# A new table for the order, the engines and the PSUM banks of all operations in a one-core recurrence and convolution kernel

## The chip, the core and the metric

The kernel runs on one core of a Trainium2 chip. The metric is the time of one execution on the device in microseconds, the median over runs. In the text PE is the matrix engine, DVE, ACT and POOL are the vector, scalar and general engines, and SP is the engine that issues the DMAs.

## The reference

Two stages, with the output of the first as the input of the second. B = 4 batches, S = 6272 steps, D = 256 channels, all in float32.

```python
def _attn_ref(x, f_logit, lower_bound):
    sig = 1.0 / (1.0 + np.exp(-f_logit))
    f = lower_bound + (1.0 - lower_bound) * sig
    h = 0
    for t in range(S):
        h = f[:, t] * h + (1.0 - f[:, t]) * x[:, t]
        y[:, t] = h

def _moe_ref(x, w_proj, filter_fft, w_out):
    x1, x2, x3 = split(x @ w_proj)                      # three times D columns
    X2 = np.fft.rfft(x2, axis=1)
    H = np.fft.rfft(filter_fft, axis=0)
    x2_conv = np.fft.irfft(X2 * H, axis=1)              # circular, of length S
    return (x1 * x2_conv * x3) @ w_out
```

## The kernel before

The Fourier transform of length 6272 = 49 x 128 is done in matmuls in two steps, with tables of sines and cosines that are computed on the chip at the start. The work of a batch has these operations; the name of an operation is the first argument of `op(...)` in the code, and the line is that of its matmul or of its main instruction.

- `load` (L308): the DMAs of 512 steps of f_logit (tile FL) and x (tile XT), 512 KB each; 13 chunks a batch, each tile with three buffers. `sig` (L311, ACT) makes the sigmoid, `u` (L313, POOL) the product with x, `su` (L325, PE) transposes both, in two operations of 16 transposes for a full chunk, `f` (L338 on ACT, L340 on DVE) makes the gate, and `scan` (L346, DVE) runs the recurrence along the chunk. `wrap` copies a part of the result for the circular access.
- `P` (L673, PE): the projection to x2 from strided columns of the recurrence's output, 13 groups; it needs all scans of the batch. `x2` evicts it.
- `F1` (L686), `mini` (L702), `F2` (L745): the two steps of the forward transform, in 16 units; `A` evicts F1, `prod` (L758, DVE) multiplies by the filter's spectrum, of which `H` (L723) loads one unit, and `slot` and `zm` do the first bin. `I2` (L768) is the first step back, and `Th` evicts it.
- `x13` (L373): 52 projections to x1 and x3, evicted by `xs`, and multiplied by `z` (L389, POOL).
- `I1` (L802): the last step back, 13 groups, which needs all `Th`; `y` (L808, DVE) multiplies by z; `proj` (L820) is the output projection, `o` evicts it, and `store` (L830) writes 512 KB.

Before the first batch the filter's own spectrum is made: 13 loads `ff`, casts `fr`, `rot` (L590), evictions `f2`, 32 `FF1` (L615) evicted by `afs`, 16 `FF2` (L633) evicted by `hw`, and stores `hst` to DRAM. The tables need two blocks of DVE work and two sines on ACT, all named `args` (L479 to L521). There are 32 operations `warm` (L561), each of four matmuls on a constant whose output is read by nothing; an operation `warm` needs only the constant and one PSUM bank.

While a batch is in F1 to I2, the scans of the next one begin; after the last I2 they go on beside I1, y and proj, and P of the next batch follows. "Cycle" b is the time from the first P of batch b to that of batch b+1.

No scheduler runs at build time. `Plan` collects 2325 operations with what they read and write; `ORDER` is a string of base-64 digits, three for each operation, in the order in which they are issued. The order on each engine, and so all waiting, follows from it: engines run their own queue in order, and semaphores hold an operation until those that it needs are done. All DMAs stand in one queue, SP's. PSUM is one tile of eight banks; the table says which bank, or pair of banks, an operation takes, and its evictions take the same.

```python
word = a * 4096 + b * 64 + c
yield word // 64, self.ENGINES[word // 8 % 8], word % 8     # operation, engine, bank
...
assert e in o["cost"] and i not in seen and o["preds"] <= seen
```

Operations with more than one engine in their `cost` (evictions, copies, gates, casts) may be given to any of these by the table.

## Time and profile before

| | |
|---|---|
| median of 3 runs | 476.47 us (476.25 to 478.01) |
| span of the profiled execution, first to last instruction | 476.4 us |
| PE busy | 447.8 us, 94% |
| DVE, ACT, POOL busy | 424.9, 416.1, 297.9 us |
| DMA | 112.88 MB, 237 GB/s on average |
| first P of batches 0, 1, 2, 3 | 78.7, 178.3, 282.7, 386.6 us |
| last F2 of batches 0, 1, 2, 3 ends | 143.6, 239.8, 346.3, 443.4 us |

The profiled execution has no separate time beside its span, which is within 0.1 us of the median, so sums may be made against either. Busy time of PE counts matmuls whose ends are modelled; a stretch in which PE is busy throughout can still hold short waits between matmuls. "Idle before" of a group is the idle time of its engine ahead of its instructions, with what ended most of it.

### The profile page before, as it was taken

How to read it: one execution, taken by the hardware profiler on the slowest of the kernel's cores; microseconds unless marked ns; L12 is line 12 of the kernel's file. 1: busy time of each engine (PE TensorE's matmuls, PEld its weight loads, DVE VectorE, ACT ScalarE, POOL GpSimd, SP SyncE). 2: the span in 40 equal slices, each digit the busy share in tenths (PEclk: the TensorE clock that was granted, in tenths of full speed). 3: DMA queues.
4: the chain of work that ended last, by engine and by line, in shares of the span. 5: the costliest groups of instructions: out<-in, count | busy, mean ns of one | idle time of the engine just before them, and what ended most of it. 6: DMA issues, size and time to landing. Idle time of an engine off the chain costs nothing.

```text
span 476.4 us, 14713 instructions
## 1 busy us (share of the span) xinstructions
PE 447.8 (94%) x6041; PEld 345.4 (72%) x6041; DVE 424.9 (89%) x457; ACT 416.1 (87%) x606; POOL 297.9 (63%) x309
## 2 busy tenths in 40 slices
PE   8888999999998999999999999999999799999995
PEld 7776777866756879776666889666767697676784
DVE  8778989799999996999999996999999877999874
ACT  5899898899999998889999978999999778999763
POOL 6777784287889730668798734688787504766600
PEclk9999999999999999999999999999999999999999
DMA  8989998636588897157769995567588831356277
GB/s 329 396 310 317 313 342 251 227 104 216 165 289 306 289 328 279 41 164 226 244 230 312 345 338 219 145 205 235 163 271 270 341 135 46 110 152 193 77 279 277
DMA packets 39841, 112.88 MB, mean 237 GB/s; under 512 B 4258, under 2 KB 6178, under 8 KB 39774
## 3 DMA queue, kind: packets, MB, share of 16 engines
q1 hardware_dynamic: 39774, 111.94, 69.0%
q8 instruction: 47, 0.77, 0.6%
q14 instruction: 20, 0.16, 0.1%
HBM read 80.93 MB, written 31.00 MB: 235 GB/s over the span
## 4 chain that ended last, share of the span: by engine, by line
PE 52%; DVE 16%; DMA 12%; POOL 6%; ACT 6%; issue 6%; SPq 0%; ACTq 0%; DVEq 0%; POOLq 0%
PE PS L373 13%; PE PS L673 9%; DVE HA L346 8%; PE PS L768 8%; PE PS L745 6%; PE PS L686 5%; DVE ys L808 5%; PE PS L325 4%; DMA XT<-in_x_dram 4%; DMA X<-in_moe_filter_fft_dram 4%; PE PS L820 3%; POOL zt L389 3%; POOL XT L313 3%; DMA out_dram<-osb 2%; DVE PP L758 2%
## 5 line engine op out<-in xcount | busy, mean ns | idle before, releaser
L389 POOL TENSOR_TENSOR zt<-x1s,x3s 128x490 f16<-128x490 f32 (+1 forms) x104 | 125.5, 1214 | 67.1 <-ACT x3s L270 33.0
L313 POOL TENSOR_TENSOR XT<-XT,FL 128x1024 f32<-128x1024 f32 (+1 forms) x52 | 116.9, 2248 | 64.7 <-ACT FL L311 41.8
L758 DVE TENSOR_TENSOR PP<-PS,Hu 98x1008 f16<-98x1008 f32 x128 | 146.5, 1198 | 4.9 <-PE PS L745 2.7
L346 DVE TENSOR_TENSOR_SCAN HA<-fTs,HA,PS 128x512 f16<-128x512 f32 (+1 forms) x96 | 112.5, 1201 | 5.1 <-ACT fTs L338 4.3
L373 PE MATMUL PS<-HA,W 128*128 128x490 f16 (+1 forms) x416 | 104.5, 368 | 1.3 <-ACT Th L270 0.6
L808 DVE TENSOR_TENSOR ys<-PS,zt 128x1024 fp32r<-128x1024 f32 (+1 forms) x52 | 58.8, 1150 | 8.5 <-PE PS L802 6.5
L820 PE MATMUL PS<-Wo,ys 128*128 128x256 f32 x392 | 57.8, 293 | 3.5 <-DVE ys L808 2.5
L270 ACT CAST HA<-PS 128x1024 f16<-128x1024 f32 x57 | 57.2, 1025 | 3.7 <-PE PS L686 3.6
L338 ACT ACTIVATE fTs<-PS,nomc 128x512 f32<-128x512 f32 (+1 forms) x86 | 56.2, 672 | 4.8 <-PE PS L325 4.3
L272 ACT ACTIVATE osb<-PS 128x1024 f32<-128x1024 f32 (+1 forms) x46 | 45.0, 985 | 16.9 <-DMA out_dram<-osb 8.7
L768 PEld LDWEIGHTS <-PP 98*128 98x128 f16 x1024 | 49.7, 98 | 11.7 <-POOL PP L750 2.1
L270 ACT COPY x3s<-PS 128x490 f32<-128x490 f32 (+1 forms) x96 | 54.6, 574 | 4.0 <-PE PS L373 1.8
L820 PEld LDWEIGHTS PS<-Wo,ys 128*128 128x128 f32 x392 | 49.3, 188 | 9.0 <-DVE ys L808 4.6
L272 ACT ACTIVATE x1s<-PS 128x490 f32<-128x490 f32 (+1 forms) x89 | 52.1, 592 | 3.9 <-PE PS L373 2.2
L373 PEld LDWEIGHTS <-W 128*128 128x128 f16 x416 | 33.4, 97 | 30.4 <-issue 8.3
L311 ACT ACTIVATE FL<-FL 128x1024 f32<-128x1024 f32 (+1 forms) x52 | 52.8, 1019 | 2.1 <-DMA FL<-in_f_logit_dram 2.0
L325 PE MATMUL PS<-iden,FL 64*128 64x64 f32 x784 | 45.8, 232 | 8.6 <-DVE HA L346 2.2
L325 PEld LDWEIGHTS PS<-iden,FL 64*128 64x128 f32 x784 | 33.7, 138 | 27.0 <-DVE HA L346 9.0
L768 PE MATMUL PS<-VA,PP 98*128 98x98 f16 x512 | 51.8, 207 | 0.6 <-POOL PP L750 0.2
L270 ACT CAST Th<-PS 128x784 f16<-128x784 f32 x61 | 50.2, 830 | 1.8 <-PE PS L768 1.2
L768 PE MATMUL PS<-VB,PP 98*128 98x98 f16 x512 | 51.6, 207 | 0.0
L673 PE MATMUL PS<-W,HA 128*128 128x256 f16 x392 | 44.6, 274 | 0.2 <-DVE HA L346 0.2
(110 smaller groups left out, 685.7 us busy)
## 6 DMA issues: line engine op xcount, KB each, us to landing
FL<-in_f_logit_dram SPq DMA_DIRECT2D x48, 512.0 KB
XT<-in_x_dram SPq DMA_DIRECT2D x48, 512.0 KB
out_dram<-osb SPq DMA_DIRECT2D x48, 512.0 KB
Hu<-H SPq DMA_DIRECT2D x55, 392.0 KB
X<-in_moe_filter_fft_dram SPq DMA_DIRECT2D x9, 512.0 KB
H<-Hu SPq DMA_DIRECT2D x16, 196.0 KB
H<-Hu SPq DMA_DIRECT2D x16, 128.0 KB
Hu<-in_moe_filter_fft_dram SPq DMA_DIRECT2D x2, 512.0 KB
```

Source lines behind the costliest of these rows:

```text
L270: nc.scalar.copy(dst, src)
L272: nc.scalar.activation(dst, src, AF.Copy, scale=scale)
L313: op("u", {"POOL": 0.1 + 0.553 * nb}, lambda e, xt=xt, ft=ft: nc.gpsimd.tensor_tensor(xt, xt, ft, op=AOP.mult), r=[("ft", k)], w=[("xt", k)])
L325: nc.tensor.transpose(bank(pb)[:, at[p] + j:at[p] + hn:nb], src[ps, j, cols], iden[ps, ps])
L346: nc.vector.tensor_tensor_scan(h, fT, bank(pb)[:, 512 - hn:512 + hn], init, op0=AOP.mult, op1=AOP.add),
L373: nc.tensor.matmul(PS[:, p, 0:n], W13[:, kh, js], HA[:, HB[kh] + t0:HB[kh] + t0 + n], start=(kh == 0), stop=(kh == 1))
L389: nc.gpsimd.tensor_tensor(late["zt"][:, jb, :, m0:m0 + nm], xs(0), xs(1), op=AOP.mult),
L673: nc.tensor.matmul(pp[:, r - r0, :], column(HB[kh], q_of(r)), W2[:, kh, :], start=(kh == 0), stop=(kh == 1))
L758: nc.vector.tensor_tensor(PP[:TB, k, o, :, :, 1:64], px.unsqueeze(1).broadcast_to([TB, 2, UE, 63]), hh[:, :, :, 1:64], op=AOP.mult)
L768: nc.tensor.matmul(PS[:, ib + o, pr * TB:(pr + 1) * TB], PP[:TB, k, o, n, 2 * pr:2 * pr + 2, :], v[:TB], start=(n == 0), stop=(n == 1))
L808: nc.vector.tensor_tensor(late["ys"][:, yk, :, 0:rn * 128], PS[:, cb:cb + 2, 0:rn * 128], late["zt"][:].rearrange("p k r m -> p k (r m)") ...
L820: nc.tensor.matmul(po[:, i, :], late["ys"][:, yk, kh, i * 128:(i + 1) * 128], Wo[:, kh, :], start=(kh == 0), stop=(kh == 1))
```

## The change

The string `ORDER` is replaced; every other line is the same (the file is two lines shorter, so that a line of the code after the table has a number smaller by 2).

```diff
 ORDER = (
-    "A8gAAYBBgAOYABIAjQBLgACIBGgAtRBQgBVgAhSBagBkgAdTA7YAPIAxUBfgA9AA2VBpgAwWBCAA0XBugBDQA+SBFABMYBzgAyUBEAARIAvV"
-    "BHYBACAqWA/CBNUA1XAQAB4gAmQERgBIRBWYAkWAcTBRAADgAYYAuXAnQBJBAgWBKBESgBSWAzTBUGBbYBXQBTGEpgAeSBYIBgYASABcSBPE"
...
+    "AAYAOYABIA7YBBgBCAA1QAfQA8gA9YAuQBLgA2QBGgBVgBQgBfgBagA5QBkgBpgBugAkQACIBDQBzgBMYA+SBFABHYBEAAPIAQAAVYAXYATIAUIB"
+    "NQBPAAWIBWIA/CBOIBIUBRABJEBKMB4gBXWBZGBgABAKBYGBSQBUABTABbIBhSBiKBqYAYYBcUBeEBlIBmQBnIBoABvIBrWBdMBjCBwQB0IByIBt"
...
 )
```

Decoded, the two tables hold the same 2325 operations. 149 of them change their engine, by kind:

| operation | engines before | engines after |
|---|---|---|
| A (F1's eviction) | ACT 57, DVE 7 | ACT 58, DVE 6 |
| Th (I2's eviction) | ACT 61, DVE 3 | ACT 63, DVE 1 |
| afs, f2, hw (start-up's evictions) | ACT 53, DVE 22 | ACT 53, DVE 22 |
| f (gate) | ACT 86, DVE 18 | ACT 91, DVE 13 |
| fr (start-up's casts) | POOL 8, ACT 4, DVE 1 | POOL 5, ACT 3, DVE 5 |
| o (output's eviction) | ACT 46, DVE 6 | ACT 51, DVE 1 |
| wrap | POOL 31, ACT 17 | POOL 43, ACT 5 |
| x2 (P's eviction) | ACT 33, DVE 19 | ACT 27, DVE 25 |
| xs (x13's eviction) | ACT 185, DVE 23 | ACT 182, DVE 26 |

1352 of the operations with banks get other banks. In the order over all engines the median operation moves by 15 places. The largest moves are those of `warm`: all 32 stood ahead of the first P; now 8 do, 20 stand between the first P and the last projection, and 4 behind that. On PE the order of su, I1, proj, F1, F2, I2 and x13 among each other changes throughout; two x13 that stood ahead of the first P come behind it. The second `args` block of DVE and the second sine of ACT come later in the start-up: the sine now stands behind the sigmoid of chunk 11, where a table load precedes it and another precedes the sigmoid that follows. On SP the input loads, the filter's stores and the spectrum's loads are ordered a little differently.

## The prediction

> **What bounds the kernel now.** I read the page first (parts 1, 2, 4), then the sums of busy time in stretches cut where the P phase of each batch begins and where its last F2 ends (times from the matmuls of L673 and L745), then the groups by form, then the timelines of the load loop and of the first 15 us.

> ```profile
> span 476.4 us, 14713 instructions
> ...
> PE 447.8 (94%) x6041; PEld 345.4 (72%) x6041; DVE 424.9 (89%) x457; ACT 416.1 (87%) x606; POOL 297.9 (63%) x309
> ...
> PEclk9999999999999999999999999999999999999999
> ...
> PE 52%; DVE 16%; DMA 12%; POOL 6%; ACT 6%; issue 6%; SPq 0%; ACTq 0%; DVEq 0%; POOLq 0%
> ```

> PE is the bound, with DVE close behind. By stretches (P to last F2, then last F2 to next P; batches 0 to 3):

> ```profile
> 91.20:143.60 52.40, 51.22 (x711) 34.55 (x709) 49.85 (x53) 49.88 (x79) 41.76 (x42) 1.00 0.62 197
> 143.60:178.30 34.70, 31.68 (x558) 26.43 (x559) 34.33 (x34) 32.55 (x49) 24.57 (x20) 1.00 0.90 305
> ...
> 239.80:282.70 42.90, 39.83 (x668) 31.34 (x663) 41.82 (x41) 40.02 (x61) 32.32 (x25) 1.00 0.87 304
> ...
> 346.30:386.60 40.30, 36.07 (x597) 29.23 (x596) 37.97 (x37) 33.93 (x51) 25.15 (x21) 1.00 0.79 281
> ```

> Columns: length, then PE, PEld, DVE, ACT, POOL busy, granted clock, DMA share, GB/s. The first row is PE-bound. In the other three DVE is busy for 34.3 of 34.7, 41.8 of 42.9 and 38.0 of 40.3 us, and PE idles 3.0, 3.1 and 4.2: scans of the next batch and y products set the pace there. The first 78.7 us (before the first P) are a start-up of their own, with DMA at a share of 0.87 to 0.96 in its 20 us windows.

> **What the change does, counted from the two tables.** No arithmetic is added. 149 operations change engine. Priced by the medians of the rows without waits, DVE's sum goes from 421.5 to 420.2 us, ACT's from 400.5 to 397.2, POOL's from 291.7 to 295.4 (12 wraps at 0.52 leave ACT). No engine's total matters to 0.5%; the order does. Four parts:

> **1. Warm-up matmuls.** Of 32 warm groups (L561) the old table has all before the first P; the new has 8 there, 4 behind the last projection, and 20 in between: 8, 4 and 8 in the three cycles from P to P, 7 of these ahead of a last F2 and 13 behind one.

> ```profile
> 8.70 1.48 PE L561 MATMUL PS<-iden 128*128 128x256 f16 x12
> ```

> Twelve take 1.48 us with the last one's own 0.27 us; so four cost (1.48-0.27)/11 x 4 = 0.44 us. 20 x 0.44 = 8.8 us more PE work after the first P. The four at the end (1.8 us) lie beside the last eviction and store: the last projection ends at 471.5 and the span at 476.4, so they cost nothing up to 4.9 us.

> **2. PE work that moves.** Between P and P the old table's matmuls, at gapless durations (x13 0.42, P 0.87, F1 0.46, F2 0.54, I2 0.70, I1 0.55, proj 1.14, su 0.62 us per operation), sum to 92.9, 98.4 and 96.2 us, and 83.1 in the last cycle: 370.6. The measured lengths are 99.6, 104.4, 103.9 and 89.8 = 397.7; take off 4.9 for the tail and PE's lost time is 22.2 us. The new table moves two x13 from the start-up into cycle 0 (+0.8) and one proj from cycle 3 to 2 (zero in sum): 97.3, 100.2, 100.8 and 82.0 without the end's warm groups = 380.3, so +9.7 with the warm groups. All of PE's order stands behind each other, so this is paid in full unless PE waits become fewer.

> **3. Waits that become fewer.** (a) The load loop: XT and FL have three buffers, so chunk c+3 is loaded only when chunk c has been transposed.

> ```profile
> 129.60 0.42 PE L325 MATMUL PS<-iden,XT 64*128 64x64 f32 x8
> 129.86 0.67 SPq L308 DMA_DIRECT2D FL<-in_f_logit_dram  x1
> ...
> 135.04 1.05 ACT L311 ACTIVATE FL<-FL 128x1024 f32<-128x1024 f32 x1
> ...
> 137.04 2.36 POOL L313 TENSOR_TENSOR XT<-XT,FL 128x1024 f32<-128x1024 f32 x1
> ...
> 139.37 0.47 PE L325 MATMUL PS<-iden,FL 64*128 64x64 f32 x8
> ```

> From 130.0 to 139.4: 9.4 us for load, sigmoid, product. The same loop takes 9.3 to 9.7 us for batch 1, about 10 for batch 2, about 11 for batch 3. PE work between the transposes of c and c+3 was 7.8, 8.1, 7.8, 7.1, 7.7 us for chunks 3 to 7 of batch 1; in the new table it is 11.1, 10.8, 10.2, 8.4, 8.6 (its warm groups among it, so they are counted once). What is short moves all that follows on PE: 1.7 at chunk 3 and 2.4 at chunk 6 make 4.1 us; with 1.5 and 2.1 for batches 2 and 3 (leads of 8.8 to 10.1) 7.7 in all. New: 1.1 + 0.3 + 1.1 = 2.5 us. (b) One-eviction waits: for each PE group I took the PE work since the group that filled its banks, or produced its operand, against the duration of that eviction plus 0.25 us (an estimate: an eviction starts about 0.04 us behind its matmul, PE about 0.06 behind its releaser, and the last matmul's own tail). Groups that fall short: 59 in the old, by 17.8 us in sum; 37 in the new, by 11.4 (0.9 of it warm groups). The gain is mostly between last F2 and next P, where the order of I1, y, proj and su is wider. The old 22.2 us = 7.7 + k x 17.8 gives k = 0.81; the new is 2.5 + 0.81 x 11.4 = 11.7, so -10.5 us. If none of it comes: 0. If lost time goes no lower than the queue work of DVE allows (the DVE queue from P to P sums to 90.7, 98.1 and 97.0, under PE's), this bound does not bite.

> **4. Start-up.** Up to its last gate, ACT's queue goes from 61.4 us and 3 table loads to 59.4 and 5, because the second sine is now queued late, between the sigmoids of chunks 11 and 12; behind it wait the last gates and so the last scans, which P needs.

> ```profile
> L521 ACT ACT_TABLE_LOAD x1 | 1.3, 1283 | 0.0
> ...
> L521 ACT ACTIVATE PP<-PP 128x512 f32<-128x512 f32 x1 | 0.7, 652 | 0.0
> ```

> 65.3 against 65.8 us with the loads; DVE 67.6 to 66.9, POOL 56.3 to 56.1, bytes ahead of the last input load one H store (0.13 to 0.2 MB) fewer. I take 0. Below: casts on POOL are 5 rather than 8 and DVE's second argument block (8.1 to 14.1 us) comes behind the casts, so FF1 (now at 24.3) can begin up to 2.5 us sooner. Above: the two loads and the sine at the late place, 3.2 us, plus 0.8 for the scans behind them: +4. [...]

> SP has the same 259 transfers and one queue; H loads and stores keep their order within a few places, with bytes unchanged: zero, its cover being DMA shares of 0.60 to 0.90 in these stretches.

> **Sum.** 476.4 + 9.7 - 10.5 + 0 = 475.6 us; the profiled span is within 0.1 of the median 476.47, so 475.6 is also the forecast of the median. A measurement of this kernel tells about 0.5% (2.4 us) from no change: faster is under 474.1, slower over 478.9.

> **Rivals.**
> PE pays, and nothing comes back. The place: last F2 to next P, where the new PE queue holds 33.1, 35.6 and 37.8 us of work and DVE's, with two products ahead, 32.1, 35.1 and 36.2 (old: PE 30.9, 39.2, 35.7; DVE 34.0, 41.5, 35.2). PE is then the bound in all three, and two equal queues wait for each other: in the old third stretch, where they are equal, 40.3 us were needed, 4.6 over the larger. The price is 0.44 us a warm group and part 2, +9.7: 486.1 us. It decides if the lost 22 us stay within 5 us of what they were. For it: lost PE time was near 6 to 8 us in each cycle, whatever the cycle's work. Against it: the loop's 9.4 us explain 4 of them.
> Waits shrink and the warm groups also fall into idle time: of the 13 behind a last F2, half (2.9 us) fit into the 10.3 us that PE idles there, and the head of the start-up gives its 2.5; with a quarter of the 9.2 us of eviction waits that I left in (0.81 x 11.4; 2.3 us): 475.6-2.9-2.5-2.3 = 467.9 us. Against it: the shortfalls already count warm groups as filler.
> The clock. The first 32 matmuls of L561 took 6.57 us, 0.205 each, against 0.11 at 8.70: PE began at half speed, and the record shows full speed from 7.3 us on. With 24 groups gone, PE between 7 and 24 us has little but 13 rotations of 0.58 us. If the clock falls and FF1, FF2 and su run at half speed until it rises, 6.8 us of PE work (24 to 32 us) doubles; half is covered by loads: +3.4, 479.0 us. [...]

> **Chances.** Forecast 0.42 (472 to 480: a third of it is faster, half the same, the rest slower); PE pays 0.30; more hidden 0.22; clock 0.06 (a third the same). Faster 0.14 + 0.22 = 0.36; same 0.22 + 0.02 = 0.24; slower 0.06 + 0.30 + 0.04 = 0.40. The range reaches from 467 (the third case's end) to 486 (the second's), leaving a tenth out on each side. The likeliest case is one of both signs; its own range is 472 to 480.

> **What would show it.** Right: the first P at 76 to 82 us; P to P lengths of about 100, 104 and 104 us with PE's idle time before su (L325) and I1 (L802) falling; five ACT table loads of 1.28 us; L561 rows at 120 to 410 us without idle time before them. Wrong: last F2 to next P longer than 34.7, 42.9 and 40.3 in sum; P to last F2 longer by over 5 us in sum than 246.8; granted clock under 1.00 between 8 and 32 us; or a start-up outside -2.5 to +4, which this working would not explain.

## The result and the profile after

| | before | after |
|---|---|---|
| median (range), us | 476.4 (476.25 to 478.01) | 483.1 (481.07 to 484.75) |
| span of the profiled execution, us | 476.4 | 479.3 |
| first P of batches 0 to 3 | 78.7, 178.3, 282.7, 386.6 | 81.4, 183.0, 286.8, 389.2 |
| last F2 of batches 0 to 3 ends | 143.6, 239.8, 346.3, 443.4 | 149.2, 250.4, 352.5, 446.0 |
| last projection ends | 471.5 | 474.3 |

The new table is slower: ratio 1.013, interval 1.0098 to 1.0162. The forecast was 475.6 us; its range (467 to 486) holds the result, its sign does not.

One thing must be known before the two profiles are compared. After's profiled execution took 481.07 us at a span of 479.3, and in every run that lists both, the time is 1.7 to 2.1 us above the span (1.9 to 2.0 for the kernel before). Before's span of 476.4 therefore fits its run of 478.01 us, not its median, as the prediction had it. So the profiles compare before's slowest run with after's fastest, and show 2.9 us (spans) of the 6.7 us between the medians. Where in the kernel the other 3.8 us lie no profile shows; the experiments below are judged by their medians.

The page of after:

```profile
span 479.3 us, 14704 instructions
...
PE 451.9 (94%) x6041; PEld 351.6 (73%) x6041; DVE 425.4 (89%) x457; ACT 415.2 (87%) x599; POOL 303.1 (63%) x318
...
PEclk9579997999999999999999999999999999999999
...
PE 60%; DVE 12%; ACT 10%; DMA 6%; POOL 6%; issue 4%; SPq 1%; ACTq 0%; DVEq 0%; POOLq 0%
```

PE is still the bound, and holds more of the chain (60% for 52%). The clock row is new: it falls in slices 2 and 3 (12 to 36 us) and again in slice 7 (72 to 84 us). Before had full speed from 7.3 to 474.9 us.

The stretches of after, P to last F2 and last F2 to P (columns as in the prediction):

```profile
81.40:149.20 67.80, 66.41 (x854) 49.51 (x854) 58.13 (x59) 62.96 (x93) 43.99 (x46) 0.98 0.65 209
149.20:183.00 33.80, 32.96 (x565) 27.19 (x560) 33.26 (x32) 31.15 (x46) 25.40 (x20) 1.00 0.85 304
...
250.40:286.80 36.40, 35.32 (x604) 29.64 (x602) 35.99 (x36) 32.73 (x49) 28.09 (x24) 1.00 0.84 302
...
352.50:389.20 36.70, 36.60 (x608) 30.66 (x604) 36.27 (x35) 32.08 (x48) 24.09 (x19) 1.00 0.75 279
```

Last F2 to next P, where the prediction looked for its gain, did shrink: 106.9 us in sum for 117.9. P to last F2 grew by as much: 257.7 for 246.8. From the first P to the last projection nothing is won or lost. The same stretch in one window, first before, then after:

```profile
78.70:471.50 392.80, 377.66 (x5269) 290.23 (x5267) 357.18 (x356) 347.83 (x506) 239.09 (x229) 1.00 0.65 219
```

```profile
81.40:474.30 392.90, 385.03 (x5356) 299.33 (x5355) 356.54 (x354) 344.88 (x499) 244.54 (x238) 1.00 0.63 220
```

PE is busy 7.4 us longer in the same length; its idle time went from 15.1 to 7.9 us. Nearly the whole difference that the profiles show, 2.7 of the 2.9 us, is there when the first P begins.

Why the first P comes late, seen from ACT and from PE in after's timeline (start, busy, instruction; in brackets the idle time before it and its releaser):

```profile
72.01 1.28 ACT L519 ACT_TABLE_LOAD   x1
73.30 0.63 ACT L519 ACTIVATE PP<-PP 128x512 f32<-128x512 f32 x1
...
74.35 0.58 ACT L268 CAST afs<-PS 128x512 fp32r<-128x512 f32 x1
...
75.53 1.28 ACT L309 ACT_TABLE_LOAD   x1
76.83 0.42 ACT L309 ACTIVATE FL<-FL 128x256 f32<-128x256 f32 x1
```

```profile
74.98 1.21 PE L613 MATMUL PS<-D1r,f 128*128 128x256 f32 x8 [1.23 <-ACT afs L268]
77.30 0.37 PE L323 MATMUL PS<-iden,FL 64*128 64x64 f32 x2 [1.11 <-ACT FL L309]
...
78.83 2.02 PE L631 MATMUL PS<-afs,FTr 64*98 64x512 f32 x8
80.66 0.81 PE L648 MATMUL PS<-mX,FTr 64*98 64x128 f32 x8
81.40 8.57 PE L671 MATMUL PS<-W,HA 128*128 128x256 f16 x66
```

The late sine and its two loads hold ACT; PE waits 1.23 us for a cast behind them and 1.11 us for the sigmoid of chunk 12, which comes at 76.8 instead of 73.3 us. The last scans, on DVE, before and after:

```profile
77.72 1.08 DVE L346 TENSOR_TENSOR_SCAN HA<-fTs,HA,PS 128x128 f16<-128x128 f32 x2 [0.27 <-ACT fTs L338]
```

```profile
77.85 2.25 DVE L344 TENSOR_TENSOR_SCAN HA<-fTs,HA,PS 128x512 f16<-128x512 f32 x3 [1.03 <-ACT fTs L336]
```

They end 1.3 us later than before, at 80.1 us, and P begins only at 81.4, behind the FF2 and `last` matmuls (L631, L648) that follow the late transposes on PE. Those run at half clock. These are windows of 3.41 us, cut where the clock changes in the record (PE busy first, granted clock third from the end):

```profile
8.73:12.15 3.42, 1.11 (x8) 0.70 (x6) 2.68 (x6) 1.91 (x4) 1.64 (x3) 1.00 1.03 414
12.15:15.56 3.41, 2.08 (x8) 1.78 (x8) 2.81 (x5) 3.26 (x6) 0.66 (x1) 0.50 1.03 411
...
73.58:77.00 3.42, 1.37 (x14) 1.03 (x10) 1.77 (x2) 3.39 (x6) 2.44 (x3) 1.00 0.82 296
77.00:80.40 3.40, 2.60 (x16) 1.80 (x18) 2.19 (x3) 2.77 (x7) 1.70 (x4) 0.50 0.38 93
80.40:83.83 3.43, 3.43 (x24) 2.63 (x21) 0.47 (x1) 2.85 (x3) 0.00 (x0) 0.50 0.84 307
```

Where PE was busy for 1.11 of 3.42 us, the next 17.1 us ran at half clock (to 29.2); where it was busy for 1.37, the next 6.8. The second stretch covers the last FF2 (2.02 us for eight matmuls, against 1.35 at full clock in a_lback2) and the head of P.

### The profile page after: what moved, and what is told of

The parts are those of the page before. It is cut to its first block, busy times and chain, and to the rows that moved or that the text cites. A ratio compares the mean times of both kernels' runs of the same rounds, so it can differ in the third digit from the quotient of the medians.

```text
span 479.3 us, 14704 instructions
## 1 busy us (share of the span) xinstructions
PE 451.9 (94%) x6041; PEld 351.6 (73%) x6041; DVE 425.4 (89%) x457; ACT 415.2 (87%) x599; POOL 303.1 (63%) x318
## 4 chain that ended last, share of the span: by engine, by line
PE 60%; DVE 12%; ACT 10%; DMA 6%; POOL 6%; issue 4%; SPq 1%; ACTq 0%; DVEq 0%; POOLq 0%
PE PS L371 14%; PE PS L671 8%; PE PS L766 8%; PE PS L684 6%; PE PS L743 6%; PE PS L818 6%; DVE HA L344 5%; DMA out_dram<-osb 5%; PE PS L323 5%; PE PS L800 3%; POOL zt L387 3%; ACT osb L270 2%; DVE PP L756 2%; POOL XT L311 2%; ACT FL L309 1%
## 5 line engine op out<-in xcount | busy, mean ns | idle before, releaser
L311 POOL TENSOR_TENSOR XT<-XT,FL 128x1024 f32<-128x1024 f32 (+1 forms) x52 | 117.1, 2253 | 62.9 <-ACT FL L309 52.5
L371 PE MATMUL PS<-HA,W 128*128 128x490 f16 (+1 forms) x416 | 101.4, 368 | 0.5 <-DVE HA L344 0.5
L336 ACT ACTIVATE fTs<-PS,nomc 128x512 f32<-128x512 f32 (+1 forms) x91 | 60.0, 678 | 4.6 <-PE PS L323 3.3
L270 ACT ACTIVATE osb<-PS 128x1024 f32<-128x1024 f32 (+1 forms) x51 | 49.6, 979 | 16.4 <-PE PS L818 7.6
L268 ACT CAST HA<-PS 128x1024 f16<-128x1024 f32 x58 | 58.6, 1024 | 2.5 <-PE PS L684 1.7
L371 PEld LDWEIGHTS <-W 128*128 128x128 f16 x416 | 35.0, 97 | 32.2 <-issue 6.9
L766 PEld LDWEIGHTS <-PP 98*128 98x128 f16 x1024 | 50.1, 98 | 10.1 <-issue 2.7
L268 ACT COPY x3s<-PS 128x490 f32<-128x490 f32 (+1 forms) x92 | 52.9, 578 | 2.1 <-PE PS L371 1.7
L268 ACT CAST Th<-PS 128x784 f16<-128x784 f32 x63 | 52.3, 830 | 1.6 <-PE PS L766 1.4
L671 PE MATMUL PS<-W,HA 128*128 128x256 f16 x392 | 46.4, 277 | 2.2 <-ACT X L268 0.9
L671 PEld LDWEIGHTS <-HA 128*128 128x128 f16 x392 | 43.6, 143 | 4.1 <-issue 2.6
```

The source lines that it names most:

```text
L268: nc.scalar.copy(dst, src)
L270: nc.scalar.activation(dst, src, AF.Copy, scale=scale)
L311: op("u", {"POOL": 0.1 + 0.553 * nb}, lambda e, xt=xt, ft=ft: nc.gpsimd.tensor_tensor(xt, xt, ft, op=AOP.mult), r=[("ft", k)], w=[("xt", k)])
L336: nc.scalar.activation(fT, sT, AF.Identity, scale=by, bias=1.0)
L371: nc.tensor.matmul(PS[:, p, 0:n], W13[:, kh, js], HA[:, HB[kh] + t0:HB[kh] + t0 + n], start=(kh == 0), stop=(kh == 1))
L671: nc.tensor.matmul(pp[:, r - r0, :], column(HB[kh], q_of(r)), W2[:, kh, :], start=(kh == 0), stop=(kh == 1))
```

## The experiments

Two candidates were put against each other: the start-up (missing warm groups and so a half clock; the late sine), and the cycles (20 warm groups that PE pays for; a worse order). Every run is compared with runs of the kernel before beside it on the same chip. Operations are moved or left out in the table only: `PLACE` says behind which operation a moved one is issued, `DROP` which are not issued, `ADD` behind which operation a warm group is issued once more. Operation 17 is the second `args` block on DVE, 18 the second sine on ACT, 26 the POOL step that uses it. The diffs show their main lines only, and where one says `old`, `new` or names groups it gives the change in words; the files hold digits and numbers.

**a_drop: the 24 late warm groups of the new table left out.**

```diff
             o = self.ops[i]
+            if i in DROP:
+                seen.add(i)
+                continue
```

> The new table, with the 24 warm groups that it places behind the first P left out (20 in the cycles, 4 at the end); 8 stay in the start-up, so the start-up is untouched. Clock theory (the loss is the granted clock of 0.50 that the new table meets from 12.1 to 29.2 us and from 77.0 to 83.8 us): 481.5 to 483.5 us, first P still near 81.4 us. Theory that PE pays for the warm groups in the cycles (0.44 us each, all on PE's path): 483.1 - 8.8 = 474 us, nearly all of it between the first P and the end. Half of each would be 478.7 us.

482.4 us (480.88 to 482.69), ratio 1.0118 (1.0097 to 1.014): within the interval of the new table. From first P to last projection:

```profile
81.20:474.20 393.00, 379.76 (x5274) 294.04 (x5272) 356.44 (x354) 345.29 (x499) 244.47 (x238) 0.99 0.63 220
```

393.0 us for 392.9, with some 80 matmuls fewer, and idle time up from 7.9 to 13.2. The warm groups lie in time in which PE waits anyway. "PE pays" falls. (a_drop's granted clock in this window is 0.99 for the new table's 1.00, so the comparison is not quite bare; h_ba, below, has neither the late groups nor a clock under 1.00 in its window, and 392.3 us.)

**a_fill and a_back: 24 warm groups into the start-up**, two behind each of the first 12 rotations; a_fill issues them in addition, a_back moves the late ones there.

```diff
-                yield word // 64, self.ENGINES[word // 8 % 8], word % 8
+                if word // 64 not in moved:
+                    yield word // 64, self.ENGINES[word // 8 % 8], word % 8
+                yield from PLACE.get(word // 64, ())
+                yield from ADD.get(word // 64, ())
```

> The new table, with 24 more warm groups (repeated, so that none is taken away elsewhere) put two each behind the first 12 rotations of the start-up. Clock theory: the granted clock stays 1.00 from 8 to 32 us, FF1 begins near 24.5 instead of 26.0 us, first P 1.5 to 3 us earlier than 81.4 us; 480 to 481.5 us; the second drop at 77 us may stay, and with it 2.5 us of the P phase. Theory that PE pays for the warm groups in the cycles: no change, 483.1 us, or slower by up to 2 us, since PE has 10.6 us more to do.

> The new table with its 24 late warm groups moved to the start-up, two each behind the first 12 rotations: both of the other two edits in one. If both causes add, its gain over the new table is the sum of theirs: by the clock theory alone 480 to 481.5 us, by the theory that PE pays alone 474 us, by both 471 to 473 us, which would be under the old table's 476.4 us and leave the rest of the new order faster than the old by 3 to 5 us.

480.04 us (478.92 to 483.37), ratio 1.0083 (1.0055 to 1.0111), and 480.22 (478.4 to 481.54), 1.0076 (1.0048 to 1.0105). The clock is 1.00 from 8 us to 78.7 and 79.5 us, then at half for one stretch of 3.4 us (from 60 to 80 us 0.97 and 0.99 in the mean, from 80 to 100 us 0.95 and 0.93). First P at 80.9 and 80.4, later than the 78.4 to 79.9 expected for a_fill; FF1 begins at 25.9 in both, so its late start in the new table (26.0 us) is not the clock's doing. So the half clock is a part of the loss, some 0.4 to 0.5% (from a_drop's or after's ratio), and by these medians not all of it: the first P is still 1.7 to 2.2 us late. The two runs differ only by the late groups, and by 0.07%: a second sign that PE does not pay for these.

**a_sine: the second sine early in the new table**, its DVE block behind the tables, itself ahead of the first sigmoid.

```diff
+PLACE = {22: ((17, 'DVE', 0),), 123: ((18, 'ACT', 0),)}
```

> The new table with the second argument block of DVE directly behind the first block's tables and the second sine of ACT ahead of the first sigmoid, so that ACT loads tables 3 times instead of 5 times; the warm groups stay as they are. If the late sine holds up the last sigmoid (chunk 12, at 76.8 us instead of 73.3) and so leaves PE idle from 73.7 to 78 us and lowers its clock through P, then first P comes 3 us earlier, the clock does not drop at 77 us, and P takes 11 us instead of 13.5: 483.1 - 5 = 478 us. If the late sine lies beside other work, 482 to 484 us; the early DVE block (5.4 us at about 7 to 13 us) may cost up to 1.5 us at the start of FF1.

483.71 us (481.21 to 484.33), ratio 1.0157 (1.0135 to 1.0179): nothing won. The DVE block now stands ahead of casts that the rotations need:

```profile
16.94 2.08 PE L597 MATMUL PS<-afs,rot 128*128 128x256 f32 x8 [6.50 <-DVE afs L282]
```

FF1 begins at 30.3 instead of 26.0 us, and the first P at 83.5. The clock does not fall at 77 us any more (1.00 from 60 to 100 us). The run moved the wait and says little about the sine's price.

**h_ba and h_ab: the two orders crossed at the first P.** The operations ahead of the first P in one table's order, then all others in the other's, with no bank changed. In h_ba the `xs` of the two x13 that the old start-up holds are issued behind the second P; in h_ab the 24 warm groups that neither part holds are left out.

```diff
-ORDER = new
+ORDER = old[:first_P] + [t for t in new if t not in old[:first_P]]
```

> The old table up to the first P, then all other operations in the order of the new table (all 32 warm groups lie ahead of the first P then; the two x13 that the old order has there stay there, with their xs evictions). Theory start-up (the whole loss is made before the first P and by the clock drop that it causes at 77 us; the new cycles cost no more than the old): first P at 78.7, full clock throughout, 474.5 to 477. Rival cycles (the 4 us that a_fill and a_back were still above the old kernel, at full clock from 5 us to 78 us, lie in the cycles): first P at 78.7, but 479 to 480.5.

> The new table up to the first P, then all other operations in the order of the old table; 24 warm groups, which the old order has ahead of the first P, are left out. Theory start-up: first P at 81.2 and half clock at 12 to 29 and 77 to 84 us as in a_drop, 480.5 to 483. Rival cycles: the old cycles are shorter than the new ones by the 4 us, so 477 to 479.

h_ba: 478.23 us (476.35 to 479.45), ratio 1.0017 (0.9994 to 1.0039), not to be told from before. h_ab: 484.96 (484.04 to 485.86), ratio 1.0164 (1.0122 to 1.0206). The loss goes with the new start-up and not with the new cycles, though h_ba lies between its two expected ranges and h_ab above both of its own (first P at 84.2). The one window for h_ba, which has no warm group behind the first P:

```profile
78.30:470.60 392.30, 377.21 (x5268) 291.85 (x5267) 356.08 (x354) 343.25 (x497) 244.59 (x238) 1.00 0.63 219
```

392.3 us with 15.1 idle, where before had 392.8 with 15.1. Half a microsecond is less than the runs of one kernel differ by, and the medians do not show it: a gain of the new cycles alone is not shown.

**a_late and a_lback: the sine behind the last gate** of batch 0, in the new table and in a_back, with the POOL step that uses it right behind it.

```diff
+PLACE = {413: ((18, 'ACT', 0), (26, 'POOL', 0))}
```

> The new table; only the second sine (and the POOL step that uses it) goes behind the last batch-0 gate's eviction instead of between the gates of chunks 11 and 12. Theory start-up, with the late sine as its last wait: the last gate at about 73 instead of 76.8, first P at 78.5 to 79.5, no drop of the clock at 77 us because PE has no gaps there, 478 to 480; the half clock of 12 to 29 us stays and costs 0.5 at most, as a_fill's first P at 80.9 against 81.4 shows. Rival (the clock of 12 to 29 us sets it): unchanged, 481.5 to 483.5, with the first P at 81. Rival (the last scans wait for PE's FF1 and FF2 work, not for the gate): first P at 80.5 to 81.4 and 481 to 483.

> As a_late, and the 24 late warm groups go into the start-up as in a_back. Theory start-up: both repairs add, first P at 78 to 79, full clock throughout, 475.5 to 478. Rival cycles: the sine gains at most 1 over a_back, 479 to 480.5.

485.68 us (484.5 to 488.71), ratio 1.0183 (1.0134 to 1.0232), and 485.22 (484.81 to 487.11), 1.0171 (1.0132 to 1.0211). All expectations missed. POOL and PE in a_late:

```profile
80.65 1.84 POOL L557 TENSOR_SCALAR ID<-PP,cols 128x256 f16<-128x256 f32 x2 [3.36 <-ACT PP L527]
82.43 0.20 POOL L630 CAST mX<-afs 128x16 fp32r<-128x16 f32 x1
```

```profile
82.69 0.93 PE L656 MATMUL PS<-mX,FTr 64*98 64x128 f32 x8 [3.79 <-POOL mX L630]
```

The step that the edit carried along stood on POOL ahead of a cast of 0.20 us, and PE waited 3.79 us for that cast. The last gates were done at 78.6 us, for 79.6 in the new table and 78.3 in the old, so the place of the sine is not what failed; the edit made a new wait of its own.

**b_drop, b_sine, b_both: each part of the new start-up alone on the old order**: the last 24 warm groups left out; the sine and its POOL step at the new place (the step ahead of the last `u`, behind the casts); both.

```diff
+DROP = the 24 last warm groups of the old order
+PLACE = {241: ((18, 'ACT', 0),), 266: ((26, 'POOL', 0),)}
```

> The old table with its last 24 warm groups left out (the first 8 stay): one part of the new start-up alone. Theory start-up, in which the half clock of 12 to 29 us costs little, because loads and evictions set the pace there (a_fill's first P came at 80.9, after's at 81.4): half clock from about 12 us, first P at 78.7 to 79.5, before +0 to +1.5 us. Rival clock (the missing warm groups are the main loss): first P at 80 or later and before +3 to +5.

> The old table with the second sine, and the POOL step that uses it, moved to the new place, between the gates of chunks 11 and 12: the other part alone. Theory start-up: two table loads and the sine are 3.2 us of ACT's queue ahead of the last gate, so the last gate comes at 76 to 76.5 instead of 73.3, PE gets gaps, first P at 81 to 82, and before +2 to +4 us; +5 or more if the clock drops at 77 us as well. Rival (ACT has slack there, the late start of FF1 makes the delay): first P at 79.5 or earlier, before +0 to +1.

> Both edits on the old table. Theory start-up: the two prices add, or more than add where PE falls to half clock again in the gaps ahead of the first P: first P at 81 to 82.5, before +3 to +6, near h_ab's ratio of 1.016. Rival (something else in the new start-up, as FF1's start at 26 instead of 24 us, is the larger part): before +0 to +2.

| | median (range), us | ratio (interval) | first P |
|---|---|---|---|
| b_drop | 480.02 (478.31 to 481.78) | 1.0080 (1.0055 to 1.0104) | 80.4 |
| b_sine | 480.90 (480.17 to 482.48) | 1.0100 (1.0069 to 1.0132) | 82.5 |
| b_both | 484.98 (482.03 to 486.73) | 1.0174 (1.0121 to 1.0227) | 85.5 |

Each costs what can be measured, and together they cost 1.74%, for a sum of 0.8 + 1.0 = 1.8; the interval of 1.2 to 2.3% leaves room on both sides. b_drop went as its rival had it (first P at 80 or later, +3 to +5 us): the expectation that the half clock costs little is refuted. b_sine's +4.5 us lies between its two figures (+2 to +4, and +5 or more with a fall of the clock); b_both's +8.5 us and first P at 85.5 lie beyond its +3 to +6 and 81 to 82.5. The windows ahead of each fall of the clock in b_drop, and in b_sine:

```profile
10.17:13.58 3.41, 0.90 (x5) 0.70 (x6) 3.20 (x15) 3.38 (x5) 2.31 (x5) 1.00 1.04 414
20.40:23.82 3.42, 2.00 (x10) 1.26 (x9) 3.07 (x6) 2.43 (x6) 1.78 (x3) 1.00 1.02 401
75.02:78.43 3.41, 2.25 (x28) 1.12 (x24) 3.27 (x4) 3.41 (x6) 2.80 (x6) 1.00 0.87 237
```

```profile
68.85:72.27 3.42, 1.67 (x23) 0.99 (x22) 3.35 (x4) 3.39 (x5) 2.48 (x2) 1.00 0.92 259
75.68:79.09 3.41, 1.56 (x20) 0.82 (x17) 2.81 (x3) 3.41 (x5) 2.41 (x4) 1.00 0.69 166
```

In b_drop the clock is halved from 13.6 to 20.4, 23.8 to 30.6 and 78.4 to 81.8 us. In b_sine the early clock is full (1.00 from 8 to 32 us), but at 70 to 80 us, where PE waits for ACT and POOL (2.4 and 1.5 us in sum from 60 to 84 us), it is halved from 72.3 to 75.7 and from 79.1 to 82.5:

```profile
69.66 1.28 ACT L530 ACT_TABLE_LOAD   x1
70.95 0.63 ACT L530 ACTIVATE PP<-PP 128x512 f32<-128x512 f32 x1
71.49 0.57 ACT L279 CAST afs<-PS 128x512 fp32r<-128x512 f32 x1
```

```profile
72.11 1.97 PE L624 MATMUL PS<-D1r,f 128*128 128x256 f32 x8 [1.70 <-ACT afs L279]
```

Eight FF1 matmuls take 1.97 us here, 1.21 at full clock. The late sine thus costs twice: by ACT's queue, and by the clock. In b_sine its POOL step costs as well: PE waits 1.00 us for the last `u` behind it, 0.50 in the new table.

**a_lback2: both repairs on the new table**, the POOL step now behind POOL's last work of the start-up, with a_back's warm groups.

```diff
+PLACE = {272: ((18, 'ACT', 0),), 292: ((26, 'POOL', 0),)}
```

> The new table with the 24 late warm groups in the start-up, as in a_back, and the second sine behind the last eviction of the start-up on ACT, with its POOL step behind POOL's last work there. In a_late and a_lback that POOL step stood ahead of a cast that PE waited for (3.79 us), which hid what the sine's move gives. Theory start-up: first P at 79 to 80, ratio to before 1.002 to 1.006. Rival (the gate's place does not matter): first P at 80.4 or later, 1.0076 or more.

478.3 us (476.2 to 479.84), ratio 1.003 (1.0008 to 1.0053): of the 1.3% some 1.0 is repaired. First P at 77.3, 1.3 us sooner than before and sooner than the 79 to 80 expected, clock 1.00 from 8 to 32 and from 60 to 100 us and 0.994 over the span, for 0.998 in before's profile. It is not faster, though: its P phase waits for ACT, where the old table's 98 matmuls ran without a gap (before, then a_lback2):

```profile
78.65 11.02 PE L673 MATMUL PS<-W,HA 128*128 128x256 f16 x98
```

```profile
82.81 2.78 PE L692 MATMUL PS<-W,HA 128*128 128x256 f16 x24 [0.67 <-ACT X L289]
87.23 1.03 PE L692 MATMUL PS<-W,HA 128*128 128x256 f16 x8 [1.64 <-ACT X L289]
```

Most of these 2.3 us come with the sine's place and not with the new order of P. In a_sine, where P has the same order at full clock and the sine lies far ahead, P waits once, for 0.42 us (first line); in a_lback2 the sine and its two loads stand on ACT among the evictions of P:

```profile
91.30 1.03 PE L680 MATMUL PS<-W,HA 128*128 128x256 f16 x8 [0.42 <-ACT X L277]
```

```profile
79.93 1.28 ACT L540 ACT_TABLE_LOAD   x1
81.22 0.63 ACT L540 ACTIVATE PP<-PP 128x512 f32<-128x512 f32 x1
81.76 1.91 ACT L289 CAST X<-PS 128x1024 f16<-128x1024 f32 x2
83.69 1.28 ACT L330 ACT_TABLE_LOAD   x1
```

**h_lb: this repaired start-up, then the old order**, to see whether those waits belong to the new cycles, and as the version that could beat both.

```diff
-ORDER = old
+ORDER = a_lback2[:first_P] + [t for t in old if t not in a_lback2[:first_P]]
```

> The start-up of a_lback2 (new order, 24 warm groups back in it, second sine behind its last eviction), then the order of the old table from the first P on. a_lback2's first P came at 77.3 us against 78.7, yet its first P phase waits 2.3 us for evictions of ACT, which the old one does not. Theory (the rest of a_lback2's loss is the new order of the first P phase): first P at 77.5 to 78.5, P gapless, ratio to before 0.995 to 0.999. Rival (it comes with the new start-up, as work that ACT still has to do after the first P, the sine and its table loads among it): P has such gaps here too, ratio 1.000 to 1.004.

483.64 us (481.56 to 485.68), ratio 1.013 (1.0105 to 1.0154). Both expectations missed, the rival by size only: the waits are there, and longer.

```profile
85.00 1.03 PE L673 MATMUL PS<-W,HA 128*128 128x256 f16 x8 [2.81 <-ACT x1s L272]
```

```profile
84.37 0.58 ACT L272 ACTIVATE x1s<-PS 128x490 f32<-128x490 f32 x1 [1.97 <-POOL ID L551]
```

The old order has an x1 eviction right behind the start-up. With the sine late, ACT reaches it only behind the sine and POOL's use of it, PE waits 2.81 us, and the 72 matmuls of P from 86.2 us on take 9.67 us, 0.134 each, for 0.112 in before (11.02 for 98). So in none of the three late places tried (a_late, a_lback2, h_lb) was the sine free. For a_lback2's last 0.3% its trace shows the waits in P and the mean clock of 0.994; what each makes of it is not settled, since h_lb brought a wait of its own. No version beat the kernel before.

## Why the prediction was wrong, by its own steps

**Parts 1 to 3 nearly cancelled, as forecast.** +9.7 and -10.5 made -0.8; the profiles give +0.1 from first P to last projection. By the prediction's own measure PE's lost time is 392.9 - 380.3 = 12.6 us, for the forecast 11.7. The rows behind part 3 came as said. First P at 81.4 lies within 76 to 82, and the P-to-P lengths are 101.6, 103.8 and 102.4 for the forecast 100, 104 and 104. The idle time before su in the same window of 95 to 474 us, before and after, and the warm groups of after:

```profile
L325 PE MATMUL PS<-iden,FL 64*128 64x64 f32 x588 | 34.8, 233 | 6.0 <-ACT osb L272 1.8 <-DVE PP L758 1.3 <-DVE HA L346 0.9
```

```profile
L323 PE MATMUL PS<-iden,FL 64*128 64x64 f32 x588 | 33.7, 231 | 0.4 <-DVE HA L344 0.2
...
L559 PE MATMUL PS<-iden 128*128 128x256 f16 x80 | 11.9, 273 | 0.2 <-ACT x3s L268 0.2
```

6.0 us became 0.4 (before I1, 2.9 became 1.6), and 80 matmuls of L559 have 0.2 us idle before them. But the two terms were not separate. They are largely the same time: with the warm groups counted as filler PE waits 7.9 us, without them 13.2 (a_drop) or 15.1 (h_ba), and the length stays. As a price of its own, 8.8 us for warm groups is too large by most of it (a_drop's ratio is 0.12% under after's, less than either interval), and most of the 10.5 us is not a gain of the order: in h_ba, whose cycles have 370.7 us of work (380.3 less 8.8 for the groups and 0.8 for two x13), PE loses 392.3 - 370.7 = 21.6 us, for 22.2 before. The sum held because the waits had been counted with the groups in them.

**Part 4, "I take 0", is the step that failed.** Its upper bound was +4, and the row was right: 3.2 us of loads and sine on ACT. The trace puts the first P +2.7 us later, and b_sine alone costs 1.0%, 4.8 us of 476.4 (3.3 to 6.3). The lower bound rested on FF1 starting sooner; it started at 26.0 instead of 24.3. Nor was the path quite the one named: the last scans came 1.3 us late, and the rest was PE's work ahead of P at half clock. Equal queue sums (65.3 against 65.8 us) were read as equal time, although the same sentence names what matters: the sine stands ahead of the last gate, which P needs, and nothing is left to hide it there.

**The clock had a chance of 0.06 and should have been a term.** What it described happened: 24 groups gone, half clock from 12.1 to 29.2 us. Its price, +3.4, is near what b_drop measured (0.8%, 3.8 us, 2.6 to 5.0), though by another way: a part is the stretch at 78 us, at the head of P, which the rival did not have. One reading of before's trace spoke against it, a granted clock of 1.00 from 470 to 474 us with PE busy for 0.95 us of 4. It was misread: the last projection ends at 471.5 us, PE is busy for 0.00 us from 471.5 to 474.9, and at 474.9, 3.4 us behind its last work, the clock falls to 0.50. In after the falls and rises in the start-up keep to steps of 3.41 us, and 1.37 us of work in 3.42 did not hold the clock.

**The sum, with both as terms:** 476.4 - 0.8 + 3.4 + 4.0 = 483.0, against 483.1. That the sizes fit so well is partly luck, since the second stretch at half clock belongs to both, and on the new table itself the repairs gave less, some 0.5% or 2.4 us each (1.3 to 0.8% in a_back, 0.8 to 0.3% in a_lback2). The prediction had each price, and left one as the end of a range and one as a rival, as if only one of the forecast, the bound and the rival could come true. They do not exclude each other, and b_both agrees with their sum.

**Rivals.** "PE pays": refuted by a_drop; it gave 486.1, near the result for the wrong reason. "More hidden": right that the warm groups fall into idle time, but part 3 had already spent that time. Table loads: five, as said, of 1.28 us, with the activation 1.29 and 1.30 us behind the load's start at the late place. "P to last F2 longer by over 5 us" and "granted clock under 1.00 between 8 and 32 us" were both named as signs of a wrong forecast, and both came.

**The span taken for the median** hid that before's profiled run was 1.6 us above its median, so a span comparison shows less than half of the loss.

## What to carry to other kernels

Price filler work and the waits that it fills as one term: compare the length of the stretch with and without it, not busy time plus idle time. A repair or a delay in a start-up should be followed to the last operation that the next phase needs; equal sums of a queue say nothing of what stands ahead of that operation. Side effects that don't exclude each other belong in the sum, each with its price, and not among the rivals.
